# Attention, experts and a gated layer in one kernel: port-aware planning of the attention order, early expert embeddings unscaled, a hinted branch, all low parts of the expert loop on VectorE

## The chip, the cores and the metric

The kernel runs on one core of one Trainium2 chip. A core has TensorE (matrix products into PSUM), VectorE, ScalarE and GpSimd for elementwise work, and SyncE, whose queue issues most DMAs. Times are device microseconds; the time of a kernel is the median of its runs. In rows of the profile PE is TensorE, PEld its weight loads, DVE VectorE, ACT ScalarE, POOL GpSimd, SP SyncE.

## The reference

Three stages follow one another, all in fp32:

```python
# 1. sliding-window attention: B, H, S, D = 4, 8, 576, 64; window 128; q, k, v
scores = (q @ k.T) / 8 - slope[h] * |i - j|      # kept for 0 <= i - j < 128, else -1e9
attn = softmax(scores)                           # with 1e-9 added to the sum
x = (attn @ v)                                   # as (2304, 512)
# 2. a mixture of 8 experts, one for each token
xn = x / (norm(x) + 1e-6); en = emb / (norm(emb) + 1e-6)
logits = xn @ en.T / tau
e = argmax(logits); gate = softmax(logits)[e]    # with 1e-9 added to the sum
x = gate * (relu(x @ w1[e]) @ w2[e])             # w1 512 x 1024, w2 1024 x 512
# 3. a second layer of 2048 columns
h = x @ w_in                                     # w_in, w_out come as 64-bit floats
g = where(h >= 1, h, where(h <= -1, 0, (h + 1)**2 / 4))
out = g @ w_out
```

The choice of the expert does not depend on the length of x or on the scale of all logits of a token, but it does depend on the length of each expert's embedding, so that length (and tau) has to be divided out before the argmax.

## The kernel before

**Splitting.** Most matrix products are made of three, of the operands' high and low parts: ScalarE rounds a tile to the high part (`qs`, `kh`, `whi`, `hh`, `xh`), and a subtraction makes the low part from the original and the rounded tile, both in SBUF (`qs`'s second half, `kl`, `wlo`) or with the original in PSUM (`hl`, `xl`). The subtractions run on VectorE or GpSimd.

**Attention (0 to about 172 us of the span).** There are 72 units: 8 groups (2 batches by 2 heads) of 9 query tiles. A unit makes scores on TensorE (`sc`, L818 and L819), adds the bias tile `mb` and finds the row maxima on VectorE (`ss`, `mx`, L831), exponentials on ScalarE (`at`, L839), transposes them (`tp`, L846), copies the transposes to SBUF on ScalarE or VectorE (`aT`, L851 and L853) and multiplies by the values (`av`, L865). Eight more columns of the values tile `vt` hold the values times the expert embeddings, which `ven_steps` (L683) makes first, so that `av` brings the logits `lpt` with it. The first group needs those embeddings before their lengths are known: it takes them unscaled (`enb0`), and `scale_first` (L928) multiplies its logits later by `esc`, one over length and tau. The other groups take the scaled ones (`enb`) that `prep_experts` makes through a chain of small VectorE steps, a scaled identity (`diag`, L734) and a product (`etp`, L739).

**What sets the order.** Within an engine instructions run in the order in which the program emits them. In attention and in the hand-over behind it that order comes from a planner in the kernel itself: each stream of steps yields what it asks for (`ask`: engines with durations in microseconds, earliest start, what must be seen before), `first_start` works out the earliest start, `drive` takes the earliest. A step that VectorE or GpSimd could do goes to the one that ends first, with 1.2 us added to VectorE (`BIAS`). The planner knows each engine's busy time, and nothing of what one engine's operation does to another's.

**Hand-over (about 172 to 203 us).** `route` finds each token's expert and place (steps L330 to L399, with the running count `cum`, L346), `gates` the gate values; rows of x are gathered by GpSimd's indirect DMAs (L1121), and the first rows of the first expert go through unsplit weights. Four subtractions of `wlo` run on GpSimd here.

**Expert loop (about 203 to 449 us).** For each of the 8 experts (in order of size) and each eighth `ff` of the 1024 columns: 12 matmuls for `bh` (L1412 to L1414), `hh` and `hl` from it, then the 12 matmuls for `by` of the step before (L1401 to L1403). Each step also converts one weight tile ahead (`convert`, L531 for the low part), transposes a quarter of the next expert's rows (`bx`, L1249; `xl`, L1244) and takes two or three steps of side work: sorting of token numbers (`poc`, `poa`, `permp`), then the 64-bit weights of the second layer (`cva`, L1014 to L1019). From the third expert on (`EPOOL`) every second weight tile's low part is made by GpSimd. In the second expert, at step 3, every engine loads the flag `anyo` and branches on it (L1430): where an expert has more tokens than its buffer holds, `overflow` takes the rest. With these inputs no engine runs that code, and the jump passes over it.

**Second layer (about 449 us to the end).** Products of split operands again, with the side work's rest ahead of them.

Of the kernel before, what the change touches and what calls it, by code (L numbers as in the profile page):

```python
# [8 lines left out]
F32 = mybir.dt.float32  # L9
# [25 lines left out]
EPOOL = 2  # L35
# [25 lines left out]
def fused_kernel(ctx, tc, qk, vT, v, emb, tau, w1, w2, win64, wout64, out):  # L61
# [96 lines left out]
    seen, rings, work = {}, {}, {}  # L158
    now, end, on, at_unit = [0.0], [0.0], ["", None], [0.0]

    def ask(engines, start=0.0, after=(), ring=None, late=None, duty=None):
        return engines, start, after, ring, late, duty

    def add(stream, rank=0.0, ready=None):
        rank_of[stream] = rank
        asks[stream] = None, now[0] if ready is None else ready, (), None, 0.0, None
        streams.append(stream)

    def first_start(s):
        engines, start, after, ring, late, _ = asks[s]  # L170
# [12 lines left out]
        e = min(engines, key=lambda e: max(start, busy[e]) + engines[e] + BIAS.get(e, 0.0) * ("G" in engines))  # L183
        start = max(start, busy[e])
        return start + late, rank_of.get(s, 0.0), e, engines[e], start

    def drive(more):
        while more():
# [16 lines left out]
            if e:  # L205
                busy[e] = end[0]
            r = next(s, StopIteration)
# [6 lines left out]
            else:  # L214
                asks[s] = None, start + r, (), None, None, None
# [15 lines left out]
    lsum = pr_.tile([P, NQ, E], F32, name="lsum", bufs=1)  # L231
    nsq = pr_.tile([P, NQ], F32, name="nsq", bufs=1)
# [80 lines left out]
    def vec(took=0.1, after=(), **k):  # L313

        return ask({"V": took}, end[0] + 0.13, after, **k)
# [4 lines left out]
    def route(i):  # L320
# [8 lines left out]
        yield ask({"V": size(1)}, after=of_tiles("lsum", c0, n))  # L329
        nc.vector.tensor_reduce(lx, ls, axis=AX.X, op=ALU.max)  # L330

# [123 lines left out]
    def root_steps(pool_, out_, s_, nm, e):  # L455
        for n, _ in enumerate(root(pool_, out_, s_, nm, nc.vector if e == "V" else nc.gpsimd)):
            yield ask({"V": 0.08} if n < 2 or e == "V" else {"G": 0.19}, end[0] + 0.13)

    def gates(pr):
# [5 lines left out]
        yield ask({"V": 0.08}, after=[("root", pr)] + of_tiles("lsum", pr * NT, NT))  # L465
# [86 lines left out]
    with ExitStack() as a:  # L552
# [14 lines left out]
        enb0 = pa.tile([P, 2, E], F32, name="enb0")  # L567
        esc = pa.tile([P, E], F32, name="esc")
        make_identity(nc, ident)
        nc.gpsimd.memset(enb0, 0.0)  # L570
# [4 lines left out]
        nc.gpsimd.affine_select(rel, rel, [[1, 256]], ALU.is_gt, 1e12, base=0, channel_multiplier=-1)  # L575
        qz = [pa.tile([P, 2, 2, P], F32R, name=f"qz{i}") for i in range(2)]
        enb = pa.tile([P, H // 2, 2, E], F32, name="enb")
# [63 lines left out]
        def split_block(g, b, h, c, cols):  # L641
# [11 lines left out]
            yield ask(of(cq.stop - cq.start, lows), end[0] + 0.13)  # L653
# [3 lines left out]
            yield ask(of(cols.stop - cols.start, lows), end[0] + 0.13)  # L657
# [949 lines left out]
```

## Time and profile before

| | us |
|---|---|
| median of 3 runs (lowest to highest) | 853.58 (846.03 to 855.09) |
| the profiled execution, its own time | 852.43 |
| its span, first to last instruction | 850.7 |
| TensorE busy | 818.7 (96%) |
| VectorE busy | 538.8 (63%) |
| ScalarE busy | 426.9 (50%) |
| GpSimd busy | 189.0 (22%) |

The span is 1.7 us shorter than the execution's own time. TensorE's busy time depends on its clock: in some stretches the granted clock is half of full speed, and the same matmuls take longer and still count as busy. So both have to be read, the idle time and the granted clock, and stretch by stretch, since the stages have different limits.

### The profile page before, as it was taken

What the parts mean: (1) busy time and instruction counts of PE and PEld (TensorE: products, weight loads), DVE (VectorE), ACT (ScalarE), POOL (GpSimd) and SP (SyncE); (2) the same over time, 40 slices, a digit from 0 to 9 for tenths busy, and PEclk for the clock granted to TensorE, in tenths of its full rate; (3) what the DMA queues carried; (4) which work ended last, traced back from release to release, by engine and by line L of the source; (5) the groups of instructions that cost most, each with busy time, mean ns of one, the idle gap of its engine ahead of it and who ended that gap; (6) DMA issues with size and microseconds to landing.
All of it is one profiled execution on the core that took longest, in us unless ns stands there. A gap on an engine that the chain in (4) does not pass through costs nothing.

```text
span 850.7 us, 14217 instructions
## 1 busy us (share of the span) xinstructions
PE 818.7 (96%) x5191; PEld 759.7 (89%) x5191; DVE 538.8 (63%) x1376; ACT 426.9 (50%) x905; POOL 189.0 (22%) x216
## 2 busy tenths in 40 slices
PE   7999999979989999999999999999999999999996
PEld 6999989967989999899999998999999898999995
DVE  7877968889657556777548999754343445444332
ACT  7789869964533455565625555433222324223222
POOL 4564543225102334353310000002000002001001
PEclk7899979989999999999999999999999999999999
DMA  8574955146744476677514344021000002000000
GB/s 324 200 271 160 333 181 180 53 138 205 229 154 146 143 258 226 203 240 249 166 40 140 121 132 124 25 75 75 1 0 1 1 10 101 3 0 34 4 1 37
DMA packets 59696, 106.05 MB, mean 125 GB/s; under 512 B 3942, under 2 KB 36710, under 8 KB 59616
## 3 DMA queue, kind: packets, MB, share of 16 engines
q1 hardware_dynamic: 56288, 95.15, 33.6%
q0 software_dynamic: 3328, 9.90, 3.3%
q8 instruction: 42, 0.69, 0.3%
q14 instruction: 38, 0.31, 0.1%
HBM read 90.42 MB, written 14.62 MB: 123 GB/s over the span
## 4 chain that ended last, share of the span: by engine, by line
issue 52%; PE 11%; POOL 4%; DVE 3%; ACT 1%; DMA 1%; POOLq 0%; ACTq 0%
POOL out L1536 2%; PE bh L1412 2%; PE by L1402 2%; PE by L1403 2%; PE by L1401 2%; PE bh L1414 2%; PE bh L1413 2%; POOL wlo L531 1%; DVE wlo L531 1%; PE bx L1249 1%; DMA raw<-in_w_in 1%; DVE cva L1016 0%; ACT whi L526 0%; DVE cva L1019 0%; ACT hh L1417 0%
## 5 line engine op out<-in xcount | busy, mean ns | idle before, releaser
L1499 DVE SCALAR_TENSOR_TENSOR r<-r 128x384 f32<-128x384 f32 x96 | 53.5, 557 | 119.7 <-ACT r L1497 119.7
L1491 PE MATMUL ch<-yh,wc_0h 128*128 128x384 f32 x384 | 129.2, 337 | 0.0
L1493 PE MATMUL ch<-yh,wc_0l 128*128 128x384 f32 x384 | 129.2, 336 | 0.0
L1492 PE MATMUL ch<-yl,wc_0h 128*128 128x384 f32 x384 | 128.8, 335 | 0.0
L1497 ACT ACTIVATE r<-ch,halfc 128x384 f32<-128x384 f32 x96 | 55.2, 575 | 117.3 <-PE ch L1493 117.1
L1519 PE MATMUL o<-wc_1l,gh 128*128 128x512 f32 x288 | 113.3, 394 | 0.0
L1518 PE MATMUL o<-wc_1h,gl 128*128 128x512 f32 x288 | 113.2, 393 | 0.0
L1502 ACT ACTIVATE gh<-r 128x384 fp32r<-128x384 f32 x96 | 50.5, 526 | 123.7 <-DVE r L1501 123.7
L1517 PE MATMUL o<-wc_1h,gh 128*128 128x512 f32 x288 | 112.0, 389 | 0.0
L1536 POOL DMA_INDIRECT out<-ot,permu x18 | 17.4, 964 | 396.9 <-ACT ot L1531 394.0
L531 POOL TENSOR_TENSOR wlo<-wraw,whi 128x1024 fp32r<-128x1024 f32 x26 | 64.1, 2469 | 104.9 <-ACT whi L526 90.0
L1402 PE MATMUL by<-hl,whi 128*128 128x256 f32 (+6 forms) x256 | 78.1, 305 | 4.0 <-DVE hl L1418 3.8
L1505 DVE TENSOR_TENSOR gl<-r,gh 128x384 fp32r<-128x384 f32 x96 | 53.5, 557 | 43.8 <-ACT gh L1502 43.8
L1412 PE MATMUL bh<-xh,whi 128*128 128x256 f32 (+6 forms) x256 | 80.7, 315 | 0.0
L1401 PE MATMUL by<-hh,whi 128*128 128x256 f32 (+6 forms) x256 | 77.9, 304 | 0.2 <-ACT hh L1417 0.2
L1414 PE MATMUL bh<-xh,wlo 128*128 128x256 f32 (+6 forms) x256 | 77.7, 304 | 0.0
L1403 PE MATMUL by<-hh,wlo 128*128 128x256 f32 (+6 forms) x256 | 77.5, 303 | 0.0
L1413 PE MATMUL bh<-xl,whi 128*128 128x256 f32 (+6 forms) x256 | 77.5, 303 | 0.0
L1491 PEld LDWEIGHTS ch<-yh,wc_0h 128*128 128x128 f32 x384 | 72.2, 188 | 2.9 <-DVE r L1501 0.4
L1492 PEld LDWEIGHTS ch<-yl,wc_0h 128*128 128x128 f32 x384 | 72.1, 188 | 2.5
L1493 PEld LDWEIGHTS ch<-yh,wc_0l 128*128 128x128 f32 x384 | 72.1, 188 | 0.0
L865 PE MATMUL av<-vt,aT 128*128 128x73 f32 (+1 forms) x576 | 66.5, 275 | 4.3 <-DVE aT L851 2.3
(269 smaller groups left out, 1834.2 us busy)
## 6 DMA issues: line engine op xcount, KB each, us to landing
wraw<-in_w SPq DMA_DIRECT2D x64, 512.0 KB, 4.0
rqk<-in_qk SPq DMA_DIRECT2D x30, 576.0 KB, 6.9
raw<-in_w_in SPq DMA_DIRECT2D x16, 512.0 KB, 3.9
raw<-in_w_out SPq DMA_DIRECT2D x16, 512.0 KB, 3.4
vT<-in_vT SPq DMA_DIRECT2D x16, 288.0 KB, 5.2
yl<-ysT SPq DMA_DIRECT2D x6, 768.0 KB, 5.2
x_dram<-xt SPq DMA_DIRECT2D x8, 512.0 KB, 5.5
vt<-in_v SPq DMA_DIRECT2D x8, 438.0 KB, 6.1
```

Of the source, the lines that this page charges most:

```text
L1401: nc.tensor.matmul(y, w2h[:, o], hh[:, :cap], start=(ff == 0), stop=False)
L1402: nc.tensor.matmul(y, w2h[:, o], hl[:, :cap], start=False, stop=False)
L1403: nc.tensor.matmul(y, w2l[:, o], hh[:, :cap], start=False, stop=(ff == 7))
L1412: nc.tensor.matmul(hp, w1h[:, o], xh[:, c, :cap], start=(c == 0), stop=False)
L1413: nc.tensor.matmul(hp, w1h[:, o], xl[:, c, :cap], start=False, stop=False)
L1414: nc.tensor.matmul(hp, w1l[:, o], xh[:, c, :cap], start=False, stop=(c == 3))
L1491: nc.tensor.matmul(hp, w1h[:, o], yh[:, c], start=(c == 0), stop=False)
L1492: nc.tensor.matmul(hp, w1h[:, o], yl[:, c], start=False, stop=False)
L1493: nc.tensor.matmul(hp, w1l[:, o], yh[:, c], start=False, stop=(c == 3))
L1517: nc.tensor.matmul(out_, gh[:, o], w2h, start=(ff == 0), stop=False)
L1518: nc.tensor.matmul(out_, gl[:, o], w2h, start=False, stop=False)
L1519: nc.tensor.matmul(out_, gh[:, o], w2l, start=False, stop=(ff == FF // P - 1))
```

## The change

- Steps of VectorE that `vec` asks for, the splits' subtractions, and the root's steps carry a mark (`port`). The planner starts a marked step of VectorE or GpSimd only when the other's marked step has ended.
- The embeddings are unscaled for all four groups of the first batch pair (`enb[0]`), and scaled ones (`enb[1]`) serve the other four. Instead of `scale_first` for the first group, `route` multiplies `lsum` of the first pair by `esc` once; `gates` waits for that. `prep_experts` gets a later rank (20 instead of 3), the bias tiles an earlier one.
- GpSimd makes the bias tiles' source `rel` ahead of the identity. Some durations that the planner assumes are changed.
- The branch is turned: the empty case is the taken one, and a hint names it as likely taken on five engines.
- `convert` in the loop takes VectorE always.

```diff
-EPOOL = 2
...
-    seen, rings, work = {}, {}, {}
+    seen, rings, work, held = {}, {}, {}, {}
...
-    def ask(engines, start=0.0, after=(), ring=None, late=None, duty=None):
-        return engines, start, after, ring, late, duty
+    def ask(engines, start=0.0, after=(), ring=None, late=None, duty=None, port=False):
+
+        return engines, start, after, ring, late, duty, port
...
-        e = min(engines, key=lambda e: max(start, busy[e]) + engines[e] + BIAS.get(e, 0.0) * ("G" in engines))
-        start = max(start, busy[e])
+        free = lambda e: max(start, busy[e], held.get({"V": "G", "G": "V"}.get(e), 0.0) if port else 0.0)
+        e = min(engines, key=lambda e: free(e) + engines[e] + BIAS.get(e, 0.0) * ("G" in engines))
+        start = free(e)
...
                 busy[e] = end[0]
+                if asks[s][6]:
+                    held[e] = end[0]
...
-        return ask({"V": took}, end[0] + 0.13, after, **k)
+        return ask({"V": took}, end[0] + 0.13, after, port=True, **k)
...
-        yield ask({"V": size(1)}, after=of_tiles("lsum", c0, n))
+        yield ask({"V": size(1)}, after=of_tiles("lsum", c0, n) + ([] if i else [("enb", 1)]))
+        if i == 0:
+
+            nc.vector.tensor_tensor(ls, ls, esc.rearrange("p (o e) -> p o e", o=1).to_broadcast(sh), op=ALU.mult)
+            yield vec(size(1))
...
-        make_identity(nc, ident)
-        nc.gpsimd.memset(enb0, 0.0)
...
+        make_identity(nc, ident)
...
-            yield ask(of(cols.stop - cols.start, lows), end[0] + 0.13)
+            yield ask(of(cols.stop - cols.start, lows), end[0] + 0.13, port=True)
...
-            yield ask({"P": 0.43}, 0.0, [("values", g, b), ("enb", min(g, 1))], "xp", duty=0.13)
+            yield ask({"P": 0.43}, 0.0, [("values", g, b), ("enb", g // (H // 2))], "xp", duty=0.13)
...
-            yield ask({"V": 0.2}, 3.1)
+            yield ask({"V": 0.35}, 2.1)
             nc.vector.tensor_scalar(mb[:, h], rel, -8.0 * 2.0 ** -(h + 1), None, op0=ALU.mult)
...
-            add(bias_of(h), 9 * (h // 2) - 3.0)
-        add(prep_experts(), 3.0)
+            add(bias_of(h), h - 20.0)
+        add(prep_experts(), 20.0)
...
+        tc.mark_branch_hint_location("overflow", hint="LikelyTaken", engines=[mybir.EngineType.PE, mybir.EngineType.DVE, mybir.EngineType.Activation, mybir.EngineType.SP, mybir.EngineType.Pool])
...
-                    with tc.If(some > 0):
+                    with tc.If(some == 0, preferred_fallthrough_block=False, label="overflow") as fits:
+                        pass
+                    with fits.Else():
                         overflow(idg)
...
-                        convert(nconv, nc.gpsimd if e >= EPOOL and nconv % 2 else nc.vector)
+                        convert(nconv, nc.vector)
```

In the built program the hint stands at the head of each engine's instructions, ahead of all of attention, not where the source marks it.

**The order at three places.** VectorE at the start of the program (`mb` are the bias tiles, `qs` and `kl` the low parts of the first loads). Before:

```order
L757 MEMSET warm 128x1
L773 TENSOR_SCALAR mb<-rel 128x256 x3
L654 TENSOR_TENSOR qs<-rqk,qs 64x256 x2
L658 TENSOR_TENSOR kl<-rqk,kh 128x256 x2
L703 COPY enb_144<-etp_222 64x8 x2
L716 TENSOR_SCALAR es_171<-es_169 8x1
```

and now:

```order
L765 MEMSET warm 128x1
L781 TENSOR_SCALAR mb<-rel 128x256 x8
L661 TENSOR_TENSOR qs<-rqk,qs 64x256
L665 TENSOR_TENSOR kl<-rqk,kh 128x256
L661 TENSOR_TENSOR qs<-rqk,qs 64x256
L711 COPY xt_143<-etp_222 64x4x8 x2
```

All eight bias tiles stand ahead of the first subtraction; the chain of the embeddings' lengths (`es`) moves to later.

VectorE around the running count `cum` of the first `route`, in attention. Before:

```order
L880 TENSOR_TENSOR lpt<-av,rs 128x2x16
L341 TENSOR_TENSOR oh_72<-fm,fl 128x8x9
L898 TENSOR_TENSOR xt_142<-av,rs 128x2x128
L346 SCALAR_TENSOR_TENSOR cum_73<-keep_74,oh_72 128x80
L851 COPY aT<-tp 128x512
L654 TENSOR_TENSOR qs<-rqk,qs 64x512
L689 COPY vt<-ep 128x8x8
L851 COPY aT<-tp 128x512
```

and now:

```order
L888 TENSOR_TENSOR lpt<-av,rs 128x2x16
L884 TENSOR_SCALAR rs<-av 128x2
L361 TENSOR_REDUCE fl<-fm 128x9
L886 RECIPROCAL rs<-rs 128x2
L351 TENSOR_TENSOR oh_72<-fm,fl 128x8x9
L888 TENSOR_TENSOR lpt<-av,rs 128x16
L356 SCALAR_TENSOR_TENSOR cum_73<-keep_74,oh_72 128x80
L839 ISA ss,mx<-sc,mb 128x256
L839 ISA mx 128x1
```

No subtraction of `qs` stands between the count and the work behind it, which is now the next unit's scores. In all of attention and the hand-over GpSimd has 28 subtractions of `qs` (before: 19) and 28 of `kl` (25), VectorE 2 (11) and 2 (5) of the same sizes; VectorE has 27 (18) of the larger products into `xt` and 5 (6) of the smaller, ScalarE 26 (60) scalings into `xt`.

VectorE in the expert loop, at the start of the fourth expert (`wlo` are low parts of weights, `cva` is side work, `hl` is what TensorE reads). Before:

```order
L1418 SCALAR_TENSOR_TENSOR hl<-bh,hh 128x314
L1451 COPY yo<-by_5610 128x344
L1451 COPY yo<-by_5612 128x344
L1418 SCALAR_TENSOR_TENSOR hl<-bh,hh 128x314
L531 TENSOR_TENSOR wlo<-wraw,whi 128x1024
L1014 TENSOR_SCALAR cva<-raw_6021 128x512
L1016 SCALAR_TENSOR_TENSOR cva<-raw_6021,cva 128x512
L1418 SCALAR_TENSOR_TENSOR hl<-bh,hh 128x314
L1019 ISA cva<-cva,cvr 128x1024
L1418 SCALAR_TENSOR_TENSOR hl<-bh,hh 128x314
```

and now:

```order
L1417 SCALAR_TENSOR_TENSOR hl<-bh,hh 128x314
L1452 COPY yo<-by_5588 128x344
L1452 COPY yo<-by_5590 128x344
L541 TENSOR_TENSOR wlo<-wraw,whi 128x1024
L1417 SCALAR_TENSOR_TENSOR hl<-bh,hh 128x314
L541 TENSOR_TENSOR wlo<-wraw,whi 128x1024
L1012 TENSOR_SCALAR cva<-raw_5999 128x512
L1014 SCALAR_TENSOR_TENSOR cva<-raw_5999,cva 128x512
L1417 SCALAR_TENSOR_TENSOR hl<-bh,hh 128x314
L541 TENSOR_TENSOR wlo<-wraw,whi 128x1024
L1017 ISA cva<-cva,cvr 128x1024
L1417 SCALAR_TENSOR_TENSOR hl<-bh,hh 128x314
```

Every step now has a `wlo` on VectorE, and GpSimd's queue behind the branch holds gathers only.

## Rows read from the trace of the kernel before

**Rows 1.** Busy time by stretch: stretch and length, then each engine's, granted clock, DMA.

```profile
0.00:30.00 30.00, 24.43 (x118) 20.19 (x119) 23.54 (x79) 19.67 (x45) 15.59 (x62) 0.72 0.86 305
...
108.00:125.00 17.00, 14.95 (x103) 14.35 (x101) 10.80 (x37) 10.26 (x27) 8.28 (x8) 0.70 0.38 132
...
172.00:203.00 31.00, 26.31 (x165) 18.88 (x165) 28.22 (x110) 15.74 (x52) 13.42 (x10) 0.89 0.47 146
203.00:267.00 64.00, 60.82 (x421) 60.12 (x420) 41.63 (x88) 31.60 (x50) 11.20 (x10) 0.97 0.61 196
267.00:430.00 163.00, 157.54 (x1123) 151.74 (x1122) 110.87 (x179) 92.25 (x160) 63.21 (x30) 1.00 0.64 206
449.00:850.70 401.70, 395.00 (x1989) 358.19 (x1987) 214.52 (x396) 139.80 (x261) 18.80 (x35) 1.00 0.14 45
```

**Rows 2.** TensorE's waits, 0 to 203: total us, times, longest.

```profile
PE tabp L394 <- DVE oap L383: 3.2, 2, 2.2
PE sc L818 <- DVE mx L831: 3.1, 5, 0.7
PE av L865 <- DVE aT L851: 2.3, 3, 1.0
...
PE etp L739 <- DVE diag L734: 1.7, 1, 1.7
```

**Rows 3.** Timeline around 110: start, length in us, operation.

```profile
109.56 1.56 DVE L346 TENSOR_TENSOR_SCAN cum<-keep,oh 128x80 bf16<-128x80 f32 x1
...
111.73 1.79 DVE L654 TENSOR_TENSOR qs<-rqk,qs 64x512 fp32r<-64x512 f32 x1
...
109.51 1.43 POOL L658 TENSOR_TENSOR kl<-rqk,kh 128x576 fp32r<-128x576 f32 x1 [0.30 <-ACT kh L656]
...
111.55 1.42 POOL L658 TENSOR_TENSOR kl<-rqk,kh 128x576 fp32r<-128x576 f32 x1
```

**Rows 4.** Timeline of the first 20 us: bias tiles, and GpSimd ahead of them.

```profile
0.84 0.20 POOL masks.py:197 MEMSET ident<- 128x128 f32 x1
...
1.43 0.34 POOL L573 IOTA rel<- 128x256 f32 x1
...
2.75 1.76 DVE L773 TENSOR_SCALAR mb<-rel 128x256 f32<-128x256 f32 x3 [1.80 <-POOL rel L575]
...
17.26 0.89 DVE L773 TENSOR_SCALAR mb<-rel 128x256 f32<-128x256 f32 x4
```

**Rows 5.** TensorE behind the branch: timeline, then busy time and clock by stretch.

```profile
245.81 0.49 PE L1249 MATMUL bx<-ident,xg 128*128 128x128 f32 x3 [3.18 <-PEq L1430]
...
245.00:250.00 5.00, 4.20 (x18) 4.23 (x19) 3.18 (x11) 1.12 (x4) 0.00 (x0) 0.71 0.38 111
250.00:255.00 5.00, 5.00 (x30) 4.97 (x30) 2.81 (x7) 1.83 (x4) 0.00 (x0) 0.95 0.34 102
```

**Rows 6.** TensorE's waits, 267 to 430.

```profile
PE by L1402 <- DVE hl L1418: 3.8, 4, 1.4
PE permp L1339 <- DVE poa L1331: 1.0, 1, 1.0
```

**Rows 7.** Groups by line, 203 to 267, then 267 to 430; last, two lines' durations over the program, ns min/median/max.

```profile
L531 DVE TENSOR_TENSOR wlo<-wraw,whi 128x1024 fp32r<-128x1024 f32 x17 | 20.7, 1223 | 8.8 <-ACT whi L526 8.2 <-PE bx L1249 0.5
...
L1019 DVE CUSTOM_DVE_ANT_0 cva<-cva,cvr 128x1024 uint16<-128x1024 uint16 x10 | 12.9, 1291 | 0.2
L1016 DVE SCALAR_TENSOR_TENSOR cva<-raw,cva 128x512 int32<-128x512 int32 x10 | 10.8, 1084 | 0.2
...
L531 POOL TENSOR_TENSOR wlo<-wraw,whi 128x1024 fp32r<-128x1024 f32 x22 | 54.7, 2486 | 99.1 <-ACT whi L526 84.2 <-DVE poa L1330 6.5 <-DVE cva L1014 5.8
...
L1019 DVE CUSTOM_DVE_ANT_0 cva<-cva,cvr x32: 675/693/2799, 314.1 to 540.4; 128x1024 uint16<-128x1024 uint16 x32
...
L1016 DVE SCALAR_TENSOR_TENSOR cva<-raw,cva x32: 678/684/2939, 310.9 to 539.7; 128x512 int32<-128x512 int32 x32
```

**Rows 8.** GpSimd's `qs` subtractions, 0 to 203, by line.

```profile
L654 POOL TENSOR_TENSOR qs<-rqk,qs 64x512 fp32r<-64x512 f32 x19 | 25.6, 1349 | 49.5 <-ACT qs L652 32.6 <-DMA rqk<-in_qk 11.2 <-DMA xt<-x_dram,tabf 4.4
```

More of the change, by code (lines that the diff above doesn't have):

```diff
@@ L157, in fused_kernel @@
     busy = dict.fromkeys("PAVGS", 0.0)
-    seen, rings, work = {}, {}, {}
+    seen, rings, work, held = {}, {}, {}, {}
     now, end, on, at_unit = [0.0], [0.0], ["", None], [0.0]
-    def ask(engines, start=0.0, after=(), ring=None, late=None, duty=None):
-        return engines, start, after, ring, late, duty
+    def ask(engines, start=0.0, after=(), ring=None, late=None, duty=None, port=False):
+        return engines, start, after, ring, late, duty, port
     def add(stream, rank=0.0, ready=None):
         rank_of[stream] = rank
-        asks[stream] = None, now[0] if ready is None else ready, (), None, 0.0, None
+        asks[stream] = None, now[0] if ready is None else ready, (), None, 0.0, None, False
         streams.append(stream)
     def first_start(s):
-        engines, start, after, ring, late, _ = asks[s]
+        engines, start, after, ring, late, _, port = asks[s]
         for e in after:
@@ L464, in gates @@
         inv = pr_.tile([P, NT], F32, name="inv")
-        yield ask({"V": 0.08}, after=[("root", pr)] + of_tiles("lsum", pr * NT, NT))
+        yield ask({"V": 0.08}, after=[("root", pr)] + of_tiles("lsum", pr * NT, NT) + ["scaled"])
         nc.vector.tensor_scalar(inv, nrm[:, cols], 1e-6, None, op0=ALU.add)
@@ L682, in ven_steps @@
                     yield ask({"P": 0.43 if i < 6 else 0.21}, duty=0.13)
-                nc.tensor.matmul(ep[:, i], keys[:, k0:k0 + P], enb[:, g % (H // 2)] if g else enb0, start=True, stop=True)
+                nc.tensor.matmul(ep[:, i], keys[:, k0:k0 + P], enb[g // (H // 2)][:, g % (H // 2)], start=True, stop=True)
             n = 6 if b else 4
@@ L696, in raw_experts @@
         def raw_experts():
[L698 to L701 removed]
+            yield ask({"P": 0.3}, after=["emb"], ring="xp")
+            etp = ps_x.tile([P, 4, E], F32, tag="xp", name="etp0")
+            for c in range(4):
+                nc.tensor.transpose(etp[:, c], embt[:, c * P:(c + 1) * P], ident[:E, :E])
+            yield ask({"V": 0.3}, end[0] + 0.2)
             for j in range(2):
[L703 removed]
+                nc.vector.tensor_copy(enb[0][j * D:(j + 1) * D, :, j], etp[j * D:(j + 1) * D])
             rings["xp"].append(end[0])
@@ L805, in unit @@
             heads = [2 * (g % (H // 2)) + j for j in range(2)]
-            yield ask({"P": 0.44 if t < 8 else 0.88}, 0.0, order("s1") + parts, "sc")
+            yield ask({"P": 0.48 if t < 8 else 0.96}, 0.0, order("s1") + parts, "sc")
             qs, kh, kl = spl[g]
@@ L855, in unit @@
             n = t % 2 if t < 8 else 0
-            yield ask({"P": 0.428 * nb}, end[0] + 0.15, order("s3") + [("ven", g, x) for x in ((0, 1) if b is None else (b,))], None if n else "av", duty=0.57)
+            yield ask({"P": 0.449 * nb}, end[0] + 0.15, order("s3") + [("ven", g, x) for x in ((0, 1) if b is None else (b,))], None if n else "av", duty=0.57)
             seen["s3", u] = end[0]
@@ L880, in finish @@
             nc.vector.tensor_tensor(lpt[:, t:t + n, 2 * hp:2 * hp + 2], av[:, :n, :, D + 1:], rs[:, :n].to_broadcast([P, n, 2, E]), op=ALU.mult)
-            scaled = end[0] + 0.13
-            if g:
-                seen["lpt", g, t] = scaled
-            else:
-                add(scale_first(t, n), 20.0, end[0])
+            seen["lpt", g, t] = scaled = end[0] + 0.13
             if hp == H // 2 - 1:
@@ L917, in finish @@
                 for i in range(n):
[L918 removed]
+                    yield ask({"A": 0.41}, ready, late=LATE[2] if pr == 0 else 0.0)
                     junk = p2.tile([P, 3 * P], BF16, tag="junk", name="junk", bufs=1)
```

33 lines of the change are left out of this document (12 added, 21 removed).

## The prediction, made before the change was run

> **What bounds the kernel now.** I read the stretches first, then in each the waits of TensorE, then the timeline around the largest. The stretches [rows 1] show TensorE busy nearly throughout: 395.0 of 401.7 us after 449 (the second layer, at granted clock 1.00, which no line of the change reaches), 157.54 of 163 us in most of the expert loop (267 to 430), less in attention (0 to 172) and the hand-over (172 to 203). [...] In 108 to 125 it was idle for 2.05 us and the clock averaged 0.70, worth 0.30 x 17 = 5.1 us. In 203 to 267 the idle time is one wait of 3.18 us. In 267 to 430 it adds up to 5.46 us. The start (0 to 30, clock 0.72) is the fourth, but its DMA share of 0.86 says that loads bound much of it.
>
> The waits [rows 2] name the engine in attention: TensorE waits for VectorE's row maxima (3.1 us, five times), for its copies of transposed attention (2.3 us) and once for the scaled identity of the expert embeddings (1.7 us). The timeline [rows 3] shows why the copies were late: the scan of L346 took 1.56 us beside a GpSimd subtraction of 1.43 us that started 0.05 us before it, and ended 0.2 us behind that; the qs subtraction on VectorE took 1.79 us beside another of 1.42 us, and ended 0.55 us behind it. Each seems held until the GpSimd one is done, and to do its own work then. The aT copy stands behind them in VectorE's queue, and TensorE behind that copy.
>
> **The change part by part.** The profiled execution took 852.43 us (span 850.7); the median of the three runs is 853.58 us, and their spread (846.03 to 855.09) is larger than most terms here. I sum against 852.43.
>
> Attention order. The planner now starts marked VectorE steps and GpSimd subtractions only when the other engine's marked step has ended. The order shows what came of it: 56 of the qs and kl subtractions on GpSimd instead of 44, nine fewer qs and three fewer kl on VectorE, nine more xt products there net of one smaller one fewer, and 34 fewer xt scalings on ScalarE. VectorE and ScalarE get lighter; GpSimd gets 12 x 1.4 us = 17 us more. At the scan nothing but small steps now stands between it and the next scores, and no subtraction ahead of the aT copy. If the engines run as planned, the event of 108 to 125 goes: 2.1 us idle and 5.1 us of clock [rows 1], together 7.2. The wait of 1.7 us for the scaled identity goes too, since that chain now runs eight score units later (the twelfth instead of the fourth), far from its only later reader: 8.9 us. This is an order made from planned durations, so real stalls can fall elsewhere; the bounds are nothing gained, and all of 8.9 plus the 3.1 us of waits for maxima (12.0).
>
> Against this, the start. All eight bias tiles now stand ahead of the first subtraction on VectorE instead of three. Beside GpSimd's constants three took 1.76 us, 0.59 each; four later took 0.89, 0.22 each [rows 4]. Five more cost 1.1 to 2.9 us, less the 0.6 us (0.84 to 1.43) by which their source rel, no longer behind the identity, starts earlier: 0.5 to 2.3 us. I take 2.3, since GpSimd's constants still run then. The attention term is -8.9 + 2.3 = **-6.6**, bounds -12 and +2.3 (a later start and nothing gained).
>
> With one answer: the five scalings of lpt go and one of lsum comes, three more tiny transposes and wider copies stand at the start, the hint is one instruction per engine; all lie on engines or at places where TensorE waits for the first loads. In the hand-over the subtractions of wlo on GpSimd are not marked, so the wait of up to 2.2 us for the routing table [rows 2] may stay, go or double; I take nothing and put 2.2 us on either side.
>
> The branch. TensorE waited 3.18 us at the sequencer for L1430, then ran at the lower level [rows 5]: 0.29 x 5 + 0.05 x 5 = 1.7 us. Waits of up to 1.4 us in the loop [rows 6] were followed by no fall: that stretch averages 1.00 [rows 1]. How much of the 3.18 us is the load of the flag and how much the far jump, no row separates; the hint can take only the latter. Bounds are 0 and 4.9 us. I take 2.5 of the wait and all of the clock, **-4.2**, because reading one word is the smaller part of such a wait as far as I can judge; the range keeps both ends.
>
> [...]
>
> The loop. Behind the branch, 22 wlo subtractions of 2486 ns on GpSimd become 22 on VectorE. Alone on VectorE one takes 1223 ns (203 to 267, with GpSimd hardly used) [rows 7], so 26.9 us come to VectorE. What goes is the time it is held: ten of L1019 average 1291 ns against a median of 693 over the program, ten of L1016 1084 against 684: 6.0 + 4.0 = 10.0 us, and more on other lines. VectorE's 110.87 us of 163 [rows 1] become at most 127.8, 78%: it doesn't become the bound on average. The holds of 2.4 us and more come apart into pieces of at most 1.22 us, and hl, which TensorE needs one ff step later, is no longer behind a hold. The waits are hl 3.8 us (four) and permp 1.0 us [rows 6]. In exchange 22 times VectorE waits for ScalarE's whi first, with xl, side work and then hl behind it, and TensorE behind hl. I leave one hl wait of mean size, 0.95 us: 4.8 - 0.95 gives **-3.9**, bounds -5.5 (all idle time of the stretch) and +2.8 (all waits stay, and two of the longest, 1.4 us, come on top). In 203 to 267, where every wlo but the first ones is on VectorE already, the branch is TensorE's only wait; that speaks for it.
>
> Sum: 852.4 - 6.6 - 4.2 - 3.9 = **837.7, say 838 us**, 1.8% under the median.
>
> **The rivals.** A measurement tells about 1% from no change here: 845.0 and 862.1 us around the median.
> - The hint does nothing: it stands at the head of each engine's program, TensorE passes its whole attention before the branch, and the jump may then wait its 3.18 us [rows 5] as before, with the half clock behind it: 837.7 + 4.2 = 842 us. For it: that distance. Against: nothing in the rows. 22%. [...]
> - The attention order gives nothing, because plan and chip drift apart and another pair collides: 837.7 + 6.6 = 844 us. For it: the plan's durations are constants, and the chip's vary (GpSimd's qs subtractions begin when ScalarE or a load lets them [rows 8], and loads share their engines). 18%.
> - Slower: GpSimd's 17 us more make the lows of q or k later than the scores that read them; TensorE idles, and its clock falls as in 108 to 125, 7.2 us each time. From 844.3, three such events give 866 us; two are within 1%, so it decides from three. Against: GpSimd idled 49.5 us ahead of its qs subtractions [rows 8], mostly until ScalarE had made the first part, so its queue has room. 8%.
> - The forecast itself: 48%. Something else, such as TensorE's ordinary fetches suffering from the armed hint, or VectorE becoming late in the loop: 4%.
>
> **How the numbers follow.** The forecast's own range is 830 (attention near -12, loop -5.5) to 847 (attention -1, branch -2). Over all cases 828 to 850 leaves out the slower rival and about a tenth at the ends. Faster by over 1%: nine tenths of the forecast, two thirds of the hint's rival, some six tenths of the third, 0.43 + 0.15 + 0.11 = 0.69. Slower: the slower rival and a little of the rest, 0.09. Within: 0.22.
>
> **What would show it.** Attention: no VectorE scan or subtraction above 1 us in 30 to 172, a granted clock of 1.00 from 30 to 172, the expert loop begins some 6 us before 203. Start: the first score matmul on a low part comes later, by up to 2.3 us. Branch: TensorE's wait for the sequencer under 1.4 us and no half clock behind it; if it is 3 us again, the hint did nothing. Loop: L1016 and L1019 at their medians, hl waits under 1 us in total. Wrong would be a prediction where a second stretch at half clock shows in attention, or where VectorE is above 90% in 267 to 430 and TensorE waits for hl more than 3.8 us.

## The result, and the profile after

The changed kernel took **842.75 us** (median of 20 runs, 840.18 to 854.47) beside 853.11 us for the kernel before (20 runs, 846.03 to 859.24): ratio 0.9898, 95% interval 0.9876 to 0.9920. The ratios here leave out runs that fell in a slower state (two of the changed kernel's 20), so they are not the quotients of the medians. Forecast were 838 us, 1.8% under the median; it is 1.0 to 1.2%. The profiled execution took 842.70 us with a span of 841.0, against 850.7 before: 9.7 us less. So the sign and the range held. The terms did not: attention, the largest of them, gave nothing, and branch and loop gave more than their forecast.

Where the 9.7 us are from is read most simply from the first and last matmul of the loop's `bh`. From the view of one tile, first the kernel before, then the changed one: line, engine, operation, count, duration in ns min/median/max, first and last start in us, forms.

```profile
L1412 PE MATMUL bh<-xh,whi x256: 277/298/682, 202.8 to 440.6; 128*128 128x256 f32 x32, 128*128 128x376 f32 x16, 128*128 128x344 f32 x16, 128*128 128x314 f32 x16
```

```profile
L1411 PE MATMUL bh<-xh,whi x256: 278/298/685, 204.0 to 430.9; 128*128 128x256 f32 x32, 128*128 128x376 f32 x16, 128*128 128x344 f32 x16, 128*128 128x314 f32 x16
```

Attention and hand-over end 1.2 us later than before (204.0 to 202.8). The loop between takes 226.9 us instead of 237.8, 10.9 us less. From its last `bh` to the end of the span are 410.1 us in both. 1.2 - 10.9 + 0.0 = -9.7.

Busy time by stretch, after (columns as in [rows 1]):

```profile
0.00:30.00 30.00, 25.42 (x124) 21.40 (x125) 18.19 (x71) 16.51 (x40) 13.98 (x61) 0.72 0.82 292
108.00:125.00 17.00, 17.00 (x171) 16.39 (x170) 14.08 (x69) 14.40 (x46) 9.54 (x10) 1.00 0.64 228
140.00:160.00 20.00, 14.91 (x102) 14.25 (x103) 11.09 (x56) 12.10 (x34) 11.91 (x23) 0.83 0.20 74
172.00:203.00 31.00, 26.37 (x177) 19.31 (x177) 28.36 (x115) 16.06 (x47) 11.92 (x9) 0.89 0.38 120
203.00:267.00 64.00, 63.55 (x442) 62.11 (x441) 43.54 (x92) 31.64 (x51) 12.65 (x11) 1.00 0.65 208
267.00:430.00 163.00, 162.33 (x1186) 157.94 (x1185) 117.53 (x205) 94.75 (x165) 7.92 (x10) 1.00 0.63 202
```

The same stretch of 140 to 160 in the kernel before:

```profile
140.00:160.00 20.00, 19.41 (x177) 18.70 (x178) 14.69 (x71) 18.77 (x59) 9.96 (x21) 1.00 0.60 217
```

Set against [rows 1]: 108 to 125 is whole now, 17.00 us busy at granted clock 1.00, so the 7.2 us that were forecast there did come. But 140 to 160, whole before, now has 5.09 us of idle time (0.59 before) and a clock of 0.83: 4.5 us more idle time and 0.17 x 20 = 3.4 us of clock, 7.9 us lost. The hand-over is as it was (26.37 busy at 0.89; before 26.31 at 0.89). The branch's stretch and the loop's are nearly whole.

TensorE's waits from 0 to 203 after, set against [rows 2] (total us, times, longest):

```profile
PE av L873 <- DVE rs L884: 4.2, 2, 3.9
PE tabp L404 <- DVE oap L393: 3.6, 2, 3.3
PE sc L826 <- DVE mx L839: 2.6, 4, 1.5
PE sc L826 <- ACT kh L663: 1.6, 1, 1.6
...
PE av L873 <- DVE aT L859: 0.8, 1, 0.8
```

The wait for the scaled identity is gone, the waits for `aT` fell from 2.3 to 0.8 us, and a new one is first: `av` for `rs`, once 3.9 us. Its timeline, VectorE, then GpSimd, then TensorE (start, length, operation, idle time before it and its releaser), and last the busy time and clock of two stretches:

```profile
138.75 1.30 DVE L125 TENSOR_SCALAR rt_yp<-rt_ip 128x9 int32<-128x9 int32 x1
...
147.22 0.18 DVE L888 TENSOR_TENSOR lpt<-av,rs 128x32 f32<-128x32 f32 x1
150.67 1.35 DVE L476 TENSOR_SCALAR inv<-nrm 128x9 f32<-128x9 f32 x1 [3.27 <-POOL nrm L141]
151.93 0.41 DVE L902 TENSOR_TENSOR xt<-av,rs 128x256 f32<-128x256 f32 x1
152.26 0.14 DVE L884 TENSOR_SCALAR rs<-av 128x4 f32<-128x4 f32 x1
```

```profile
141.87 1.43 POOL L665 TENSOR_TENSOR kl<-rqk,kh 128x576 fp32r<-128x576 f32 x1
143.28 0.28 POOL L127 TENSOR_SCALAR rt_ip<-nsq 128x9 f32<-128x9 f32 x1
...
146.31 1.27 POOL L661 TENSOR_TENSOR qs<-rqk,qs 64x512 fp32r<-64x512 f32 x1
...
147.94 1.26 POOL L661 TENSOR_TENSOR qs<-rqk,qs 64x512 fp32r<-64x512 f32 x1
...
149.62 0.45 POOL L677 TENSOR_TENSOR qz<-rqk,qz 64x128 fp32r<-64x128 f32 x1
...
150.43 0.20 POOL L141 TENSOR_TENSOR nrm<-rt_yp,nsq 128x9 f32<-128x9 f32 x1
150.59 1.40 POOL L665 TENSOR_TENSOR kl<-rqk,kh 128x576 fp32r<-128x576 f32 x1
```

```profile
141.09 0.39 PE L826 MATMUL sc<-kh,qs 128*128 128x256 f32 x1 [1.54 <-DVE mx L839]
...
152.49 3.66 PE L873 MATMUL av<-vt,aT 128*128 128x73 f32 x16 [3.89 <-DVE rs L884]
...
150.00:155.00 5.00, 2.52 (x12) 2.55 (x13) 3.38 (x9) 1.85 (x6) 3.21 (x5) 0.58 0.00 0
155.00:160.00 5.00, 5.00 (x34) 4.97 (x34) 2.27 (x18) 1.72 (x5) 0.00 (x0) 0.73 0.02 3
```

GpSimd's root of the first batch pair starts behind a burst of low parts and is cut into by three more (`qs`, `qs`, `qz`), so that it takes from 143.28 to 150.63. VectorE's `inv`, the first step of `gates`, stands in VectorE's queue ahead of `xt` and `rs`. It waits 3.27 us, then takes 1.35 us beside GpSimd's next `kl` of 1.40 (the other `inv`, at 190.5 with GpSimd idle, takes 0.17), and everything behind it waits along: `xt` and `rs` read the two `av` buffers, and TensorE's next `av` starts 0.09 us after `rs` has ended. TensorE is idle 3.89 us, and its clock falls: 0.58 in 150 to 155, 0.73 in 155 to 160, and 0.50, the half clock, in each microsecond from 151 to 157 (before, from 114 to 124). Most of the rest of the 5.09 us is a smaller wait of the same root: its step `rt_yp`, which VectorE makes before GpSimd's part begins, took 1.30 us beside a GpSimd `kl` of 1.45 us (from 138.56), and TensorE waited 1.54 us for a row maximum that stands behind it in the queue.

The branch and the loop, after: TensorE's first matmul behind the branch and the two stretches, then its waits in 267 to 430, then three groups of VectorE there ([rows 5 to 7]).

```profile
244.44 0.49 PE L1248 MATMUL bx<-ident,xg 128*128 128x128 f32 x3 [0.45 <-PEq L1429]
...
245.00:250.00 5.00, 5.00 (x32) 4.97 (x31) 4.14 (x13) 2.31 (x4) 0.00 (x0) 1.00 0.32 107
250.00:255.00 5.00, 5.00 (x36) 4.97 (x35) 3.38 (x9) 1.89 (x3) 0.00 (x0) 1.00 0.31 108
```

```profile
PE bx L1248 <- ACT xg L1297: 0.3, 1, 0.3
PE by L1401 <- DVE hl L1417: 0.2, 1, 0.2
```

```profile
L541 DVE TENSOR_TENSOR wlo<-wraw,whi 128x1024 fp32r<-128x1024 f32 x43 | 52.6, 1223 | 14.2 <-ACT whi L536 14.2
...
L1017 DVE CUSTOM_DVE_ANT_0 cva<-cva,cvr 128x1024 uint16<-128x1024 uint16 x10 | 6.9, 688 | 0.2
L1014 DVE SCALAR_TENSOR_TENSOR cva<-raw,cva 128x512 int32<-128x512 int32 x10 | 6.9, 687 | 0.2
```

The branch's wait is 0.45 us instead of 3.18, with no half clock behind it (1.00 in 245 to 255; before, 0.50 in 248 to 250). The side work's two lines are at their medians (1291 and 1084 ns before), and TensorE's waits for `hl` are 0.2 us instead of 3.8.

### The profile page after: what moved, and what is told of

Read it like the earlier page. It is cut to its first block, busy times and chain, and to the rows that moved or that the text cites. A ratio compares the mean times of both kernels' runs of the same rounds, so it can differ in the third digit from the quotient of the medians.

```text
span 841.0 us, 14144 instructions
## 1 busy us (share of the span) xinstructions
PE 816.4 (97%) x5195; PEld 757.7 (90%) x5195; DVE 529.9 (63%) x1390; ACT 419.4 (50%) x871; POOL 145.8 (17%) x206
## 4 chain that ended last, share of the span: by engine, by line
issue 55%; PE 11%; POOL 2%; DVE 1%; ACT 1%; DMA 0%; POOLq 0%; ACTq 0%
POOL out L1537 2%; PE bh L1411 2%; PE bh L1413 2%; PE bh L1412 2%; PE by L1400 2%; PE by L1402 2%; PE by L1401 2%; PE bx L1248 1%; DMA wraw<-in_w 0%; ACT whi L536 0%; DVE wlo L541 0%; POOL gap L1536 0%; POOL xg L1119 0%; PE permp L1338 0%; ACT yo L1450 0%
## 5 line engine op out<-in xcount | busy, mean ns | idle before, releaser
L541 DVE TENSOR_TENSOR wlo<-wraw,whi 128x1024 fp32r<-128x1024 f32 x60 | 73.3, 1223 | 20.6 <-ACT whi L536 20.1
```

## The experiments

The **theory**: branch and loop are the whole gain; the new attention order removes one stretch at half clock and makes another, where VectorE stands before GpSimd's root. The **rival**: attention gave its 6.6 us and the rest gave less than the trace seems to say. Ratios are to runs of the kernel before on the same chip. Loop begin and loop length are the first start of `bh`, and the time to its last, in the profiled execution. That is one run among several and not always a typical one: for loop alone, for branch and loop, and for the root seen later it took 4 to 6 us longer than the median, for attention alone 4 us less.

| | median us | ratio, 95% interval | loop begins | loop length |
|---|---|---|---|---|
| before | 853.11 | 1 | 202.8 | 237.8 |
| changed | 842.75 | 0.9898 (0.9876 to 0.9920) | 204.0 | 226.9 |
| branch alone | 851.73 | 0.9993 (0.9961 to 1.0025) | 206.2 | 234.1 |
| loop alone | 847.41 | 0.9937 (0.9905 to 0.9968) | 208.2 | 231.5 |
| attention alone | 855.46 | 1.0044 (1.0009 to 1.0078) | 201.3 | 238.2 |
| branch and loop | 838.51 | 0.9844 (0.9796 to 0.9892) | 205.7 | 227.2 |
| changed, root seen later | 835.21 | 0.9823 (0.9778 to 0.9868) | 200.9 | 227.8 |
| changed, root on VectorE | 839.82 | 0.9895 (0.9840 to 0.9950) | 198.9 | 227.6 |
| changed, no marks | 846.53 | 0.9951 (0.9921 to 0.9981) | 207.4 | 227.4 |
| changed, no hint | 847.94 | 0.9974 (0.9939 to 1.0008) | 202.0 | 232.8 |
| root seen later, hand-over on VectorE | 833.29 | 0.9815 (0.9785 to 0.9845) | 194.9 | 227.9 |
| branch, loop and marks | 832.15 | 0.9817 (0.9786 to 0.9847) | 192.8 | 227.4 |
| branch, loop, hand-over on VectorE | 840.09 | 0.9891 (0.9849 to 0.9932) | 195.4 | 227.6 |
| changed, durations of before | 847.98 | 0.9948 (0.9919 to 0.9978) | 209.1 | 227.9 |

### One part at a time

Branch alone: the kernel before with

```diff
+        tc.mark_branch_hint_location("overflow", hint="LikelyTaken", engines=[...])
-                    with tc.If(some > 0):
+                    with tc.If(some == 0, preferred_fallthrough_block=False, label="overflow") as fits:
+                        pass
+                    with fits.Else():
                         overflow(idg)
```

> The kernel before with the turned and hinted branch alone. Theory (the gain of the changed kernel is the branch and the loop; attention gave nothing): TensorE's wait at the branch falls from 3.18 us to about 0.4 us and the half clock behind it goes, together 4.5 us: about 848 us beside 852.4, ratio 0.995. Rival (attention gave its 6.6 us as forecast, and the branch only shifted work): the branch wait shrinks but the later stretches give it back, ratio 1.000. Every other stretch reads as before in both.

TensorE's only wait in 203 to 267, and its stretch behind the branch (11.82 us busy at 0.89 before):

```profile
PE bx L1250 <- PEq L1431: 0.4, 1, 0.4
```

```profile
240.00:255.00 15.00, 14.55 (x87) 14.24 (x87) 9.31 (x23) 8.40 (x13) 0.00 (x0) 1.00 0.48 160
```

In the trace the theory holds for the branch: the loop is 3.7 us shorter, and from its last `bh` to the end it is 410.1 us as before. The time did not show it: 0.9993 is the rival's number, and the interval (from 0.9961) leaves out 3.7 us (0.9957), if narrowly. In the profiled execution the loop begins 3.4 us later than before, with the same order of instructions ahead of it, so what the rival put behind the branch lies ahead of it here. More on that at the end.

Loop alone: the kernel before with

```diff
-                        convert(nconv, nc.gpsimd if e >= EPOOL and nconv % 2 else nc.vector)
+                        convert(nconv, nc.vector)
```

> The kernel before with every low part of the expert loop on VectorE, and nothing else. Theory: the waits of TensorE in 267 to 430 (hl 3.8 us, permp 1.0 us, 5.46 us idle in all) fall to under 1 us, 4.8 to 5.2 us gained, ratio 0.994; the branch wait of 3.2 us stays. Rival (the loop's holds on VectorE mattered less than the branch's state ahead of it): under 2 us, ratio above 0.998.

TensorE's stretch in the loop, of this kernel:

```profile
267.00:430.00 163.00, 162.33 (x1168) 157.78 (x1167) 119.72 (x214) 94.58 (x163) 10.72 (x13) 1.00 0.67 213
```

Idle time falls from 5.46 to 0.67 us and the loop is 6.3 us shorter, ratio 0.9937: the theory, a little more than it said. The branch still costs 3.3 us here.

Attention alone: the changed kernel without the two edits above.

```diff
+EPOOL = 2
...
-        tc.mark_branch_hint_location("overflow", ...)
...
-                    with tc.If(some == 0, preferred_fallthrough_block=False, label="overflow") as fits:
-                        pass
-                    with fits.Else():
+                    with tc.If(some > 0):
...
-                        convert(nconv, nc.vector)
+                        convert(nconv, nc.gpsimd if e >= EPOOL and nconv % 2 else nc.vector)
```

> The kernel before with the new attention order (marks, unscaled embeddings, bias tiles first) and neither the new branch nor the new loop. Theory: the stretch at half clock of 108 to 125 goes, another of the same size comes at 145 to 160, where VectorE stands before GpSimd's root steps; the loop begins 0 to 1.5 us later than before, ratio 1.000 to 1.002. Rival (what was forecast: 6.6 us in attention, and the loop and branch gave less than the trace seems to say): 846 us, ratio 0.992.

```profile
PE av L874 <- DVE rs L885: 4.3, 2, 3.9
PE tabp L405 <- DVE oap L394: 3.6, 2, 3.3
```

These are TensorE's largest waits up to 203 there: the same event again, 3.9 us. The ratio is 1.0044, above 1 with its interval. The rival, 0.992, is out.

Branch and loop together, with the attention of before (both diffs of above):

> The kernel before with branch and loop, and the attention order of before. Theory: both gains add, 9.5 us: about 843 us, ratio 0.989, the same as the whole change or up to 1.2 us better. Rival (attention's new order is a real gain): 849 us, ratio 0.996, 6 us slower than the whole change.

838.51 us, ratio 0.9844: a larger gain than the theory's (0.989, at the interval's edge). The loop is 10.6 us shorter, where the two alone gave 3.7 + 6.3 = 10.0: they add. The whole change is at 0.9898; the two intervals overlap a little (0.9876 to 0.9892), and both comparisons (this one, and attention alone) say that the new attention order costs some 0.4 to 0.5%, that is 4 to 5 us: more than the 1.2 us of the profiled execution. On top of the loop's edit the branch shows in the time too: 0.9937 to 0.9844, with intervals clear of each other.

### Is it the root that VectorE waits for?

The planner takes GpSimd's root as seen later, so that `inv` stands later in VectorE's queue, behind the next scores; GpSimd's order is the same to the last instruction:

```diff
-        seen["root", pr] = end[0] + 0.13
+        seen["root", pr] = end[0] + (5.0 if e == "G" else 0.13)
```

> The changed kernel, but the planner takes the GpSimd root of the first batch pair as seen 4.9 us later, so that the step inv, which reads it, and the gate steps behind it come later in VectorE's queue; GpSimd's order is the same. Theory (VectorE stood 3.3 us before GpSimd's root at 147.4 to 150.7 with xt and rs behind it, TensorE then 3.9 us without a free av buffer, and its clock fell): the wait of av for rs goes from 4.2 us to under 1 us and the clock of 140 to 160 from 0.83 to 1.00, 3.9 + 3.4 = 7.3 us at most: 836 us beside 842.7, ratio to before 0.980. Rival (GpSimd's late low parts are the bound there, kl ends at 153.4, and the next scores read it): TensorE waits for kl instead, under 2 us gained, ratio 0.987.

```profile
140.00:160.00 20.00, 17.50 (x150) 17.11 (x149) 14.14 (x74) 16.16 (x46) 11.93 (x22) 0.91 0.22 81
```

```profile
PE av L873 <- DVE rs L884: 0.3, 1, 0.3
...
142.39 0.58 PE L826 MATMUL sc<-kh,qs 128*128 128x256 f32 x1 [2.27 <-DVE mx L839]
```

835.21 us, ratio 0.9823, its interval wholly under the changed kernel's. The wait of `av` for `rs` is 0.3 us, and VectorE's order is the same up to `inv`. One line that moves `inv` and the gate steps behind it gives back 0.75%, 6.4 us (by the ratios, since the two kernels ran on different chips): the cause is shown. GpSimd's late low parts, the rival, were not the bound. Part of the loss stays in the profiled execution (busy 17.50, clock 0.91, where 1.00 was expected): a wait of 2.27 us for a row maximum at 142, behind two small VectorE steps (`nsq` and `rt_yp`) that took 1.43 and 1.12 us beside GpSimd's low parts.

The root on VectorE instead:

```diff
-        e = "V" if pr == NP - 1 else "G"
+        e = "V"
```

> The changed kernel with the root of the first batch pair on VectorE instead of GpSimd: ten small steps there instead of thirteen on GpSimd. Theory: the same gain as a later inv, less some 2 us of VectorE's time, most of it hidden: 836 to 838 us, ratio 0.981, no wait of av for rs above 1 us, and GpSimd's kl of 150.6 ends 4 us earlier. Rival (the lows are late whatever the root does): 841 us or more, ratio 0.987.

839.82 us, 0.9895 (0.9840 to 0.9950), from 835.30 to 846.56 in six runs. The gain that the theory expected (0.981) is not there: the ratio is the changed kernel's, though the interval is wide. The wait for `rs` is gone here too (0.3 us), and one of 3.5 us for a row maximum is there instead.

### What of the attention edits helps, and what costs

The planner ignores the marks; all else as changed:

```diff
-        free = lambda e: max(start, busy[e], held.get({"V": "G", "G": "V"}.get(e), 0.0) if port else 0.0)
+        free = lambda e: max(start, busy[e], held.get({"V": "G", "G": "V"}.get(e), 0.0) if False else 0.0)
```

> The changed kernel with marks that the planner ignores; unscaled embeddings, early bias tiles, branch and loop stay. Theory (the marks moved the held steps, and with them GpSimd's lows and root to a later time): VectorE steps above 1 us come back beside GpSimd's in 30 to 172, the wait of inv for GpSimd's root shrinks or goes, 838 to 842 us. Rival (the later embeddings and the bias tiles first cause the event): the half clock at 140 to 160 stays and the holds come on top, 846 us or more, ratio 0.993.

```profile
PE sc L826 <- DVE mx L839: 5.1, 5, 1.7
PE av L873 <- DVE aT L859: 4.9, 3, 3.7
```

846.53 us, slower than with the marks. The held `qs` subtractions are back on VectorE (1.50, 1.49 and 1.44 us at 82, 104 and 124), `inv` meets its root without a wait, and TensorE waits for maxima and `aT` instead. Neither expectation fits whole: the event at 140 to 160 did go, and the time is the rival's.

The marks alone, on branch and loop with the embeddings, bias tiles and assumed durations of before:

```diff
-        e = min(engines, key=lambda e: max(start, busy[e]) + engines[e] + BIAS.get(e, 0.0) * ("G" in engines))
-        start = max(start, busy[e])
+        free = lambda e: max(start, busy[e], held.get({"V": "G", "G": "V"}.get(e), 0.0) if port else 0.0)
+        e = min(engines, key=lambda e: free(e) + engines[e] + BIAS.get(e, 0.0) * ("G" in engines))
+        start = free(e)
...
+                if asks[s][6]:
+                    held[e] = end[0]
...
```

> The kernel before with branch, loop and the marks, but the scaled embeddings, bias tiles and assumed durations of before. Theory (the marks alone end the holds, and the rest of the attention edits is what costs): 832 to 837 us beside 838.5 for branch and loop alone, ratio below 0.982. Rival (the marks are what pushes GpSimd's root and lows late, as in the changed kernel): a wait of TensorE behind VectorE's inv or behind a late low part of over 2 us, 841 us or more, ratio above 0.987.

```profile
30.00:171.00 141.00, 137.77 (x1301) 133.04 (x1300) 106.17 (x550) 126.61 (x341) 75.08 (x78) 1.00 0.58 208
```

```profile
L469 DVE TENSOR_SCALAR inv<-nrm x2: 164/169/174, 151.0 to 179.2; 128x9 f32<-128x9 f32 x2
...
  POOL nrm L142: 0.2, 1
```

**832.15 us**, with 831.98 to 834.00 in five runs the narrowest of all. From 30 to 171 this is the attention that the prediction described: the clock is 1.00, no VectorE step there takes over 1 us (one of 2.22 us follows at 171.61), and `inv` (the lines above: its durations, and the idle time of VectorE ahead of it) waits 0.2 us for the root. In the same 141 us the records count 1301 matmuls, against 1235 before and 1214 after the whole change, and the loop begins 10 us earlier than before. Run beside it on the same chip, branch and loop with the old order (and the hand-over's low parts moved, below) had 0.9891 with an interval that just clears this one, and its fastest run (834.56) is slower than the slowest here (834.00). With the marks taken out of the changed kernel (0.9951 for 0.9898, above) this speaks for a gain by the marks; against branch and loop without that move (0.9844, another chip) the intervals overlap.

That leaves the edits that this kernel lacks. The changed kernel with four assumed durations of before differs from it by the embeddings and the bias tiles alone:

```diff
-            yield ask({"P": 0.48 if t < 8 else 0.96}, 0.0, order("s1") + parts, "sc")
+            yield ask({"P": 0.44 if t < 8 else 0.88}, 0.0, order("s1") + parts, "sc")
...
-            yield ask({"P": 0.449 * nb}, ...)
+            yield ask({"P": 0.428 * nb}, ...)
...
-                    yield ask({"A": 0.59}, ready, so_far("xt"), late=LATE[2])
+                    yield ask({"A": 0.51}, ready, so_far("xt"), late=LATE[2])
...
-                    yield ask({"A": 0.41}, ready, ...)
+                    yield ask({"A": 0.3}, ready, ...)
```

> The changed kernel with four assumed durations of before (scores 0.44 and 0.88 instead of 0.48 and 0.96, av 0.428 instead of 0.449, squares 0.51 and 0.30 instead of 0.59 and 0.41 us); marks, unscaled embeddings and early bias tiles stay. It differs from marks with the old embeddings (832.2 us) by embeddings and bias tiles alone, and from the changed kernel (842.7) by the four durations alone. Theory (the changed durations made the plan drift, so that VectorE met GpSimd's root 3.3 us early): no wait of av for rs above 1 us, 832 to 836 us, ratio 0.982. Rival (the unscaled embeddings, whose extra scaling and wait for it stand ahead of the gates, make the drift): a wait of 3 us or more before GpSimd's root or another held step stays, 840 us or more, ratio above 0.988.

```profile
126.07 1.21 DVE L376 TENSOR_SCALAR ki_all<-key_all 128x9 int32<-128x9 f32 x1
...
129.46 1.51 DVE L393 TENSOR_TENSOR oap<-eqp,tokhi 128x216 bf16<-128x216 bf16 x1
130.89 1.47 DVE L390 TENSOR_SCALAR ocp<-rowi,lo_all 128x128 bf16<-128x128 bf16 x1
```

```profile
PE av L873 <- DVE aT L859: 5.5, 1, 5.5
```

847.98 us, 0.9948: the theory about the durations is wrong. With them as before the kernel is no faster than the changed one; it looks slower, with intervals that touch. The root's wait goes, and another chain meets GpSimd's burst of low parts: three steps of `route` are held to 1.2 to 1.5 us, with the `aT` copies behind them, and the table of waits puts 5.5 us there. Against the marks with old embeddings (0.9817) the unscaled embeddings and early bias tiles cost 1.3% here. Which of these two does it, and by which step, was not tried.

### The hint, and the hand-over

The branch turned, no hint, so that the wait shows which of the two shortens it:

```diff
-        tc.mark_branch_hint_location("overflow", hint="LikelyTaken", engines=[...])
...
-                    with tc.If(some == 0, preferred_fallthrough_block=False, label="overflow") as fits:
+                    with tc.If(some == 0, preferred_fallthrough_block=False) as fits:
```

> The changed kernel with the branch turned and no hint. [...] Rival (turning the branch is enough): the wait stays at 0.4 us, 843 us.

```profile
PE bx L1247 <- PEq L1428: 3.2, 1, 3.2
```

```profile
240.00:255.00 15.00, 11.84 (x56) 11.52 (x55) 6.50 (x17) 3.88 (x6) 0.00 (x0) 0.77 0.29 95
```

847.94 us, the loop 5.9 us longer than the changed kernel's; the ratio, 0.9974 (0.9939 to 1.0008), is clear of that kernel's. The wait is back at 3.2 us with a fall of the clock behind it (0.77 in 240 to 255, 1.00 with the hint): the hint does it, and turning alone leaves the wait as it was.

The four low parts of the hand-over on VectorE, once on the changed kernel with the later `inv`, once on branch and loop with the old order:

```diff
-            yield ask({"G": 2.31}, max(end[0] + 0.13, base + u), [("lo", j - 1)] if j else [])
-            convert_lo(i, nc.gpsimd, i + NRAW < 8)
+            yield ask({"V": 1.15}, max(end[0] + 0.13, base + u), [("lo", j - 1)] if j else [])
+            convert_lo(i, nc.vector, i + NRAW < 8)
```

> The changed kernel with the root seen 4.9 us later, and with the four low parts of the hand-over on VectorE too (asked for with 1.15 us). Theory (in the hand-over two wlo on GpSimd held two VectorE steps of the root to 2.25 and 2.27 us between the count and the table, and a third held a gate step to 2.94 us; TensorE waited 2.5 us for the table): two wlo of 1.2 us in that place instead of 4.2 us of holds, and the gate step at 0.2 us with one of 1.2 us ahead: 1.8 + 1.5 = 3.3 us less to the loop at most, 832 to 834 us beside 835.2, ratio to before 0.979. Rival (VectorE is busy 26 of 30 us there, so its own 4.9 us cost as much as the holds): 835 to 837 us, ratio 0.983.

> The kernel before with branch and loop, and the four low parts of the hand-over on VectorE. Theory: as with the other attention order, 1 to 3 us less than branch and loop alone (838.5): 836 us, ratio 0.981. Rival (the holds of the hand-over are hidden there, since the wait of tabp was 2.2 us only, or VectorE's own time takes their place): 838 to 840 us, ratio 0.985.

Inconclusive. In the first the wait for the table, 2.5 us without this edit, is gone, and its medians are 833.29 and 835.21; but the ratios, 0.9815 and 0.9823, are within each other's intervals. In the second the ratio is 0.9891, above 0.9844 without the edit, again within the intervals. Two kernels beat the changed one clearly: marks with old embeddings, and the changed kernel with the root seen later, with or without this edit.

## Why the prediction was right, and where it was not

**Attention (-6.6 forecast, +1.2 in the traces, some +4 by the times).** This step failed, in one of its parts. The event of 108 to 125 went (7.2 us, as costed) and so did the wait for the scaled identity (1.7 us). The 8.9 us were then booked as if nothing could take their place, though the text itself said that stalls could fall elsewhere. One did: -7.2 - 1.7 + 7.9 = -1.0. The +1.2 lies within the term's bounds, which reached to +2.3, but those had been made of a later start and nothing gained, and that is not what happened; and the time of attention alone, 0.4% over that of before, is 3.8 us (0.8 to 6.6), above the upper bound in its middle. Up to the loop's begin TensorE is idle for 16.7 us in both traces, at a mean clock of 0.92 in both: what the new order took away at 108 came back later. The remaining 2.2 us to +1.2 are not placed; the loop's begin differs by more than that between executions of one and the same attention order (202.8 to 208.2 in the table). The sign by which it would be wrong was named, a second stretch at half clock in attention, and it is there. Its mechanism is near that of the slower rival: GpSimd's added subtractions make something late. But it was the root, which VectorE waits for, not a low part for TensorE, and there was one event of 7.9 us instead of three of 7.2. The outcome is that of the rival in which the attention order gives nothing because another pair collides: it gave 844 us and 18%. Why VectorE comes to `inv` 3.3 us before the root stays open; restoring the assumed durations moved the collision and did not end it.

**The held steps.** Forecast was no VectorE scan or subtraction above 1 us in 30 to 172, and there is none. But other steps are held: four (`lsum` 1.22, `fm` 1.50, `rt_yp` 1.30 and `inv` 1.35 us) where seven steps of all kinds were. The plan keeps them apart only as far as the chip keeps to the plan. It does in the kernel with marks and old embeddings, where no step of VectorE in 30 to 171 took over 1 us.

**The start (+2.3 taken).** Too dear. Eight bias tiles took 2.36 us, 0.295 each, where 0.59 was taken:

```profile
2.36 2.36 DVE L781 TENSOR_SCALAR mb<-rel 128x256 f32<-128x256 f32 x8 [1.32 <-POOL rel L581]
```

The first subtraction behind them starts at 4.75 instead of 4.54, the first score matmul on a low part at 6.18 instead of 5.82. The first scores' step on VectorE comes at 10.57 instead of 8.04, but TensorE is not idler in 0 to 30 (busy 25.42 to 24.43, clock 0.72 in both).

**The branch (-4.2).** Right: 2.7 us of wait (3.18 to 0.45) and the 1.7 us of clock go, 4.4; that 2.5 of the wait would go was an estimate that no row shows. The loop's length says 3.7 (branch alone), 4.3 (added to the loop's edit) and 5.9 (hint taken away), the last with a clock that fell lower (0.77 in 240 to 255, 0.89 before). By the time it is nothing for branch alone, 0.9% on top of the loop's edit and 0.8% where the hint was taken away; why the first differs is open. The rival that the hint does nothing is out. Without the hint the wait is 3.2 us, with it 0.4; by what means the hint does it no trace shows.

**The loop (-3.9).** Right in its mechanism, too small: -6.3 alone, -6.9 on top of the branch. No `hl` wait of 0.95 us stayed. I had also counted only TensorE's own waits (4.8 us). Its weight loads waited for `hl` besides, 5.6 us in seven times before and 0.7 in two after; they overlap with the matmuls ahead of them (157.94 us of weight loads beside 162.33 of matmuls in the 163 us after), and how much of them is in the rest of 1.5 to 2.1 us was not tried apart.

**The sum.** Branch and loop gave 10.9 us for 8.1 forecast, attention and hand-over -1.2 for 6.6: 9.7 instead of 14.7. The range held since it had been made to reach the case in which attention gives nothing; that the total came within 5 us of the forecast is in part luck, since one term was too hopeful and another too small. The upper end of the forecast's own range does not follow from its terms: attention -1 and branch -2 with the loop's -3.9 make 845.5, not 847.

## What to carry to other kernels

An order that keeps two engines' colliding steps apart is worth what the chip keeps of its plan: after such a change look first for a step that waits for another engine at the head of an in-order queue, and for what stands behind it; give such a step slack in the plan (here `inv`, which waited 3.27 us). When an edit removes an event of half clock, don't book it without a row that says that the neighbouring stretches have room. And test the parts of a planner's change alone: here the marks seem worth keeping, and the edits that came with them took it back.

## What the runs showed of the hardware

- **A hinted branch.** The hint stands at the head of each engine's program (the trace of the changed kernel has it at 0.78 to 0.90 us), some 240 us ahead of the branch, and still cut the wait from 3.2 to 0.4 us.
- **Tiny steps are held too.** A VectorE step on 128 x 9 values (`inv`) took 1.35 us beside a GpSimd subtraction of 1.40, and 0.17 us in the other `inv` of the changed kernel, with GpSimd idle (0.16 and 0.17 in marks with old embeddings). `fm` on 128 x 72 took 1.50 us, begun 0.03 us after a GpSimd `kl` of 1.44; the step behind it on as many values (L346, at 113.71) took 0.20.
- **The same order, different times.** Before, branch alone, loop alone, and branch and loop have the same attention, instruction for instruction. Their profiled executions begin the loop at 202.8, 206.2, 208.2 and 205.7 us. They differ early in attention: in 0 to 30 the clock is 0.72, 0.65, 0.77 and 0.83 and the DMA share 0.86, 0.81, 0.84 and 0.84, and the wait for the scaled identity is 1.7, 1.7, 3.9 and 5.0 us. This may be what hides the branch's 3.7 us in its own time, though twelve runs stand behind that; it was not shown. It is why one profiled execution is not enough to price a change of a few microseconds ahead of the loop.
